# Strassen's form for the second products of the second MLP of a fused attention and MLP kernel

## The chip, the cores and the metric

The kernel runs on one core of one Trainium2 chip. The metric is the device time of one execution in microseconds. All of the work, from the inputs in HBM to the result in HBM, is one launch.

## The reference, cut to what matters

The change is in the last step of the reference. x comes from an attention step and a first MLP and has 4 batches of 576 tokens with 512 features each. The weights of the second MLP are w_ch1 (512 x 1536) and w_ch2 (1536 x 512); w_tok1 and w_tok2 mix the tokens ahead of it.

```python
def _moe2_ref(x, w_tok1, w_tok2, w_ch1, w_ch2):
    xt = x.transpose(0, 2, 1)
    h = np.maximum(xt @ w_tok1, 0.0) @ w_tok2
    u = x + h.transpose(0, 2, 1)
    h2 = np.maximum(u @ w_ch1, 0.0) @ w_ch2
    return (u + h2).astype(np.float32)
```

## The kernel before, in words

**Tiling.** The 2304 tokens are 18 tiles of 128 and 9 chunks of two tiles (CT = 2, CN = 256 tokens). The chunks are numbered 0 to 8 in the first MLP and 9 to 17 in the second (NCH = 9), so chunk 9 is the first one of the second MLP. The hidden features are cut into units of 128: 16 units per chunk in the first MLP (UA), 12 in the second (UB). `seq` lists all units in order as pairs (chunk, unit).

**Precision.** An operand of a product is held as two fp32r numbers, a high part and the low part that is left, and a product is three matmuls: high by high, high by low, low by high (PASSES). In the tiles the index of the part is 0 for high and 1 for low.

**One unit.** `g1(i)` (L875) makes the unit's 128 hidden features for 256 tokens: 4 blocks of input features by 3 passes, 12 matmuls of 256 columns into a bank of PSUM ("h", two banks). `relu(i)` (L884, ScalarE) writes the high part, `low(i)` (L888, VectorE) the low part into the tile "ht". `g2(i)` (L901) multiplies them by the unit's 128 rows of w_ch2: 2 tiles of tokens by 3 passes, 6 matmuls of 512 columns, which add to two banks `acc[c, 0]` and `acc[c, 1]` over the 12 units of the chunk. `chunk_end` adds the banks to u (`evac`, L914, VectorE) and stores the two tiles.

**Order.** Up to unit 111 the order of all instructions is written out by hand. Behind it, from the later part of the first MLP on, the loop at the end of `block_kernel` emits for each unit i: `g1`, `relu`, `low` of unit i+1, then what was `put` at unit i, then `g2(i)`. A planner with a simulated timeline then sets the order of each engine's instructions from that; each engine and the DMA queue of SP run them in that order.

**Work around the units.** `w_load` and `w_split` bring the second MLP's weights (double precision in HBM, "st", L298) and convert them (L257 to L275) one unit ahead of chunk 9's use; `put_tok` places a batch's token products: `xs_load` (L970, a DMA of a tile of x into the tile xr), `xs_split` (L976 ScalarE, L977 GpSimd, into the tile xs), `tok1` (L992), `tok_relu` (L1001, L1002). `put_prep2` places `u_load`, `tok2` (L1023, added to u in L1028) and the turning of u into the operand of `g1` (L810, L818, L830, L835). `close_att` gives the attention's memory to the pools of this part.

Of the kernel before, what the change touches and what calls it, by code (L numbers as in the profile page):

```python
# [197 lines left out]
def block_kernel(ctx: ExitStack, tc: tile.TileContext, qk, vw, vh, vg, g_ln, wa, t1, t2, wb, band, near, lv, edge, out):  # L198
# [24 lines left out]
    ident = const.tile([128, 128], F32, name="ident")  # L223
    identr = const.tile([128, 128], F32R, name="identr")
    maskr = [const.tile([128, NTL, k], F32R, name=f"maskr{k}") for k in (KW, KB)]
    grow = const.tile([128, DM], F32, name="grow")
# [706 lines left out]
    PW = 512 + 3 * 64

    def load_tok(i):
        if i == 0:
            tokw["t1"] = tok["pool"].tile([128, 2, NTL, DT], F32R, tag="t1w", name="t1w")
            tokw["t2"] = tok["pool"].tile([128, 2, 2, PW], F32R, tag="t2w", name="t2w")
            for a in range(2):
                nc.vector.memset(f32(tokw["t2"][:, a, :, 512:576]), 0.0)  # L940
# [56 lines left out]
    def tok_relu(b):  # L997
        r = wp.tile([128, DT // 128, 2, DM], F32R, tag="w", name="r")
# [13 lines left out]
    def tok2(c, j):  # L1012
# [323 lines left out]
```

## Time and profile before

| | |
|---|---|
| time, three runs | 885.16, 886.54, 889.37 us (median 886.54) |
| time of the profiled execution | 886.56 us |
| its span, first to last instruction | 884.8 us |
| TensorE busy | 863.8 us (98%), 6418 matmuls |
| VectorE busy | 518.4 us (59%) |
| ScalarE busy | 251.4 us (28%) |
| GpSimd busy | 193.6 us (22%) |
| mean granted clock of TensorE | 0.998 |

Busy time is the union of an engine's instructions. PE is TensorE's matmuls, PEld its weight loads, DVE is VectorE, ACT ScalarE, POOL GpSimd, SP the engine that issues the DMAs. A name with q is the engine's sequencer, which waits or issues. L875 is line 875 of the kernel. In an instruction, out<-in are the names of the tiles. Matmuls overlap, so that the time from start to start is less than the duration of one.

### The profile page before, as it was taken

The page shows a single profiled execution, that of the slowest core. Times are in us where ns is not written, and L with a number is a line of the kernel's source. Part 1 is how long each engine was busy: PE and PEld are TensorE (multiplying, and loading weights), DVE is VectorE, ACT ScalarE, POOL GpSimd, SP SyncE. Part 2 cuts the span into 40 slices and gives each one's busy share as a digit, 9 for nine tenths or more (in the row PEclk, how much of TensorE's full clock was granted, in tenths as well). Part 3 has the DMA queues.
Part 4 walks back from the last instruction along what each step waited for, and adds up shares of the span by engine and source line. Part 5 has one row for each costly group of instructions (what it writes and reads, how often), then busy time and mean ns, then how long its engine had stood idle before and what let it go on. Part 6 is the DMA issues. An engine that isn't in the chain of part 4 may idle for free.

```text
span 884.8 us, 16767 instructions
## 1 busy us (share of the span) xinstructions
PE 863.8 (98%) x6418; PEld 766.3 (87%) x6418; DVE 518.4 (59%) x1114; ACT 251.4 (28%) x713; POOL 193.6 (22%) x197
## 2 busy tenths in 40 slices
PE   7999999999999999999999999989999999999998
PEld 6888899887989999989999887879898898999997
DVE  5999999999998776832222779863213232222221
ACT  5665535354322111322111233222121111111111
POOL 7731323566873510111000000110010000000000
PEclk9999999999999999999999999999999999999999
DMA  9747776578662522532111356632222121121100
GB/s 280 193 151 225 225 237 199 148 199 224 168 150 72 139 49 60 175 92 89 36 37 48 107 155 178 193 115 53 52 56 46 29 67 35 17 45 23 31 24 24
DMA packets 126752, 98.39 MB, mean 111 GB/s; under 512 B 78744, under 2 KB 104376, under 8 KB 126672
## 3 DMA queue, kind: packets, MB, share of 16 engines
q1 hardware_dynamic: 126672, 97.31, 39.4%
q8 instruction: 51, 0.84, 0.4%
q14 instruction: 29, 0.24, 0.1%
HBM read 72.87 MB, written 16.53 MB: 101 GB/s over the span
## 4 chain that ended last, share of the span: by engine, by line
PE 66%; DVE 19%; DMA 8%; SPq 3%; issue 2%; POOL 1%; ACT 1%; DVEq 0%; ACTq 0%; POOLq 0%
PE h L875 30%; PE acc L901 27%; DMA xr<-x_scr 3%; DMA st<-in_wb_dram 3%; SPq L818 3%; PE k L901 2%; DVE cv L267 2%; PE g L1023 2%; DVE ht L888 1%; DVE cv L262 1%; DVE lp L718 1%; DVE la L726 1%; DVE cv L257 1%; PE k L992 1%; DMA up_scr<-od 1%
## 5 line engine op out<-in xcount | busy, mean ns | idle before, releaser
L875 PEld LDWEIGHTS h<-xt,w 128*128 128x128 f32 x3024 | 394.2, 191 | 22.9 <-DVE ht L888 2.1
L875 PE MATMUL h<-xt,w 128*128 128x256 f32 x3024 | 404.8, 284 | 1.4 <-DVE ht L888 1.3
L901 PE MATMUL acc<-w,ht 128*128 128x512 f32 x1416 | 367.7, 395 | 3.0 <-DVE ht L888 2.4
L901 PEld LDWEIGHTS acc<-w,ht 128*128 128x128 f32 x1416 | 253.5, 189 | 52.3 <-DVE ht L888 4.6
L888 DVE SCALAR_TENSOR_TENSOR ht<-h,ht 128x256 fp32r<-128x256 f32 x252 | 105.6, 419 | 273.4 <-ACT ht L884 273.0
L884 ACT ACTIVATE ht<-h 128x256 fp32r<-128x256 f32 x252 | 96.7, 384 | 439.0 <-PE h L875 355.8
L977 POOL TENSOR_TENSOR xs<-xr,xs 128x512 fp32r<-128x512 f32 x20 | 26.5, 1323 | 293.3 <-ACT xs L976 293.3
L272 ACT ACTIVATE w<-cv 128x512 fp32r<-128x512 f32 x56 | 35.5, 635 | 66.6 <-DVE cv L267 66.5
L684 POOL TENSOR_TENSOR lp<-lqk 128x576 f32<-128x576 f32 x28 | 40.4, 1444 | 43.2 <-DVE ls L690 31.5
L275 DVE TENSOR_TENSOR w<-cv,w 128x512 fp32r<-128x512 f32 x56 | 42.8, 767 | 4.3 <-ACT w L272 4.1
L267 DVE SCALAR_TENSOR_TENSOR cv<-st,cv 128x512 int32<-128x512 int32 (+4 forms) x63 | 44.2, 703 | 0.4
L655 POOL TENSOR_TENSOR x<-x,et 128x256 f32<-128x256 f32 (+2 forms) x40 | 32.0, 820 | 50.6 <-DMA et<-loc_scr 40.0
L262 DVE SCALAR_TENSOR_TENSOR cv<-st,cv 128x512 int32<-128x512 int32 (+4 forms) x63 | 41.5, 659 | 0.4
L257 DVE TENSOR_SCALAR cv<-st 128x512 int32<-128x512 int32 (+4 forms) x63 | 27.3, 433 | 15.2 <-DMA st<-in_wb_dram 10.5
L455 POOL TENSOR_TENSOR vg<-vg 72x256 f32<-72x256 f32 x39 | 31.4, 806 | 18.3 <-DMA vg<-in_vg_dram 15.3
L992 PE MATMUL k<-xs,t1w 128*128 128x512 f32 (+1 forms) x120 | 32.1, 406 | 2.6 <-ACT xs L976 1.9
L1023 PE MATMUL g<-r,t2w 128*128 128x512 f32 x120 | 34.0, 394 | 0.0
L830 ACT ACTIVATE xt<-xt 128x512 fp32r<-128x512 f32 x30 | 18.9, 631 | 34.6 <-DMA xt<-xc 31.2
L835 DVE TENSOR_TENSOR xt<-xt 128x512 fp32r<-128x512 f32 x30 | 24.1, 803 | 7.3 <-ACT xt L830 7.0
L901 PE MATMUL k<-w,ht 128*128 128x512 f32 x96 | 26.0, 403 | 0.1
L992 PEld LDWEIGHTS k<-xs,t1w 128*128 128x128 f32 (+1 forms) x120 | 19.2, 188 | 7.9 <-ACT xs L976 2.8
L1023 PEld LDWEIGHTS g<-r,t2w 128*128 128x128 f32 x120 | 20.9, 189 | 3.0
(189 smaller groups left out, 656.4 us busy)
## 6 DMA issues: line engine op xcount, KB each, us to landing
st<-in_wa_dram SPq DMA_DIRECT2D x28, 512.0 KB
st<-in_wb_dram SPq DMA_DIRECT2D x24, 512.0 KB
xt<-xc SPq DMA_DIRECT2D x480, 16.0 KB
qk<-in_qk_dram SPq DMA_DIRECT2D x13, 581.0 KB
x_scr<-x SPq DMA_DIRECT2D x18, 256.0 KB
x<-x_scr SPq DMA_DIRECT2D x9, 512.0 KB
out_dram<-x SPq DMA_DIRECT2D x18, 256.0 KB
xr<-x_scr SPq DMA_DIRECT2D x16, 256.0 KB
```

The lines of the kernel that those rows point to most:

```text
L257: return nc.vector.tensor_scalar(out=f, in0=h, scalar1=3, scalar2=0x3FFFFFFF, op0=ALU.logical_shift_left, op1=ALU.bitwise_and)
L262: nc.vector.scalar_tensor_tensor(out=f, in0=h, scalar=-0x40000000, in1=f, op0=ALU.bitwise_and, op1=ALU.bitwise_or)
L267: nc.vector.scalar_tensor_tensor(out=f, in0=l, scalar=29, in1=f, op0=ALU.logical_shift_right, op1=ALU.bitwise_or)
L272: nc.scalar.activation(out=hi, in_=f.bitcast(F32), func=ACTF.Copy)
L275: nc.vector.tensor_tensor(out=lo, in0=f.bitcast(F32), in1=f32(hi), op=ALU.subtract)
L684: nc.gpsimd.tensor_tensor(out=t["pr"], in0=t["qk"][:, :VQ], in1=t["qk"][:, VQ + D * o:VQ + D * o + VQ], op=ALU.mult)
L875: nc.tensor.matmul(out=hp[:, :CN], lhsT=w[:, 0, a, kk * 128:(kk + 1) * 128], rhs=xT[c][:, kk, e, :], start=(n == 0), stop=(n == 3 * KD - 1),)
L884: nc.scalar.activation(out=t[:, 0], in_=hps[i][:, :CN], func=ACTF.Relu)
L888: nc.vector.scalar_tensor_tensor(out=t[:, 1], in0=hp[:, :CN], scalar=0.0, in1=f32(t[:, 0]), op0=ALU.max, op1=ALU.subtract)
L901: nc.tensor.matmul(out=acc[c, j], lhsT=t[:, a, j * 128:(j + 1) * 128], rhs=w[:, 1, e, :], start=(m == 0 and n == 0), stop=(last and n == 2),)
L992: nc.tensor.matmul(out=rps[b, m], lhsT=tokw["t1"][rows, a, n, m * 128:(m + 1) * 128], rhs=t[rows, e, :], start=(n == 0 and i == 0), stop=( ...
L1023: nc.tensor.matmul(out=ps, lhsT=tokw["t2"][:, a, m, o:o + 128], rhs=r_t[b][:, m, e, :], start=(i == 0), stop=(i == len(ops) - 1),)
```

## The change

In the second MLP, from chunk 10 on, units 1 to 10 are taken as five pairs. With A the four blocks of relu(u w_ch1) (two tiles of tokens by two units) and B the four blocks of w_ch2 (two units by two halves of 256 output features), the eight block products of a pair become the seven of Strassen's form (as Winograd wrote it): four of A's operands and four of B's are sums of blocks. Units 0 and 11 of a chunk, and all of chunk 9, stay as they are.

`tq_sums` makes the sums of B once for each pair, beside chunks 9 and 10; `pair_sums` makes those of A for each pair of each chunk and splits all seven operands into high and low; `g1_pair` makes both units' first products in one bank; `g2_pair` makes the seven products, which add to the two banks acc and, for the four that belong to more than one output block, to two banks of "g"; `mix` adds these two banks to u at the end of the chunk. To make room, constants of the attention move into its pool, xr is dropped (a load goes into the second half of the tile xs and is split in place), the buffers of x and u are shared out anew, `tok_relu` reuses two tiles, the zero columns of the token weights get narrower, `tok2` uses the banks "k", and batches 2 and 3 of the token products are placed three units later.

The diff, cut to its core:

```diff
+FAST = 11
+QF = DM // 2
...
     def relu(i):
-        hT[i] = t = ht_p.tile([128, 2, CN], F32R, tag="ht", name="ht")
+        if i < base[NCH + 1]:
+            t = ht_p.tile([128, 2, CN], F32R, tag="ht", name="ht")
+        else:
+            t = tok["h2"].tile([128, 2, 7, 128], F32R, tag="h7", name="h7", bufs=2)
+            t = t[:, :, :2].rearrange("p e j n -> p e (j n)")
+        hT[i] = t
...
+    def fast(i):
+        c, m = seq[i]
+        return c > NCH and 0 < m < FAST
+
+    def tq_open():
+        for k in range(2):
+            t = wp.tile([128, 4, 2, QF], F32R, tag="w", name="tw")
+            free.extend(t[:, q] for q in range(3 + k))
+            if k == 0:
+                nc.vector.memset(f32(t[:, 3, 1]), 0.0)
+                z = t.rearrange("p q e n -> p (q e) n")
+                tq["z"] = [z[:, 0::7], z[:, 2::5]]
...
+    def tq_sums(m):
+        b = []
+        s = tok["pool"].tile([128, 2, DM], F32, tag="xs", name="ts", bufs=2)
+        for k in (m, m + 1):
+            w = wt[UA + k]
+            t = s[:, k - m]
+            nc.vector.tensor_copy(t[:, 0:1], gate[0])
+            nc.gpsimd.tensor_tensor(out=t, in0=f32(w[:, 1, 0]), in1=f32(w[:, 1, 1]), op=ALU.add)
+            b.append(t)
+        (b11, b12), (b21, b22) = ((t[:, :QF], t[:, QF:]) for t in b)
+        for o, x, y in ((b11, b12, b11), (b12, b22, b12), (b22, b22, b11), (b21, b21, b22)):
+            nc.vector.tensor_tensor(out=o, in0=x, in1=y, op=ALU.subtract)
...
+        tq[m] = [wt[UA + m][:, 1, :, QF:]] + [free.pop(0) for _ in range(3)]
+        for t, v in zip(tq[m], (b11, b22, b12, b21)):
+            nc.scalar.activation(out=t[:, 0], in_=v, func=ACTF.Copy)
+            nc.vector.tensor_tensor(out=t[:, 1], in0=v, in1=f32(t[:, 0]), op=ALU.subtract)
+
+    def g1_pair(i):
+        hp = ps_h.tile([128, 2, CN], F32, tag="h", name="h")
+        for k in range(2):
+            c, m = seq[i + k]
+            w = wunit(c, m)
+            for n, (kk, a, e) in enumerate([(kk, a, e) for kk in range(KD) for a, e in PASSES]):
+                nc.tensor.matmul(
+                    out=hp[:, k], lhsT=w[:, 0, a, kk * 128:(kk + 1) * 128], rhs=xT[c][:, kk, e, :],
+                    start=(n == 0), stop=(n == 3 * KD - 1),
+                )
+        hps[i] = hp
+
+    def pair_sums(i):
+        hp = hps.pop(i)
+        t = hT[i] = tok["h2"].tile([128, 2, 7, 128], F32R, tag="h7", name="h7", bufs=2)
+        f = tok["h2"].tile([128, 7, 128], F32, tag="hf", name="hf")
+        for k in range(2):
+            nc.scalar.activation(
+                out=f[:, 2 + 2 * k:4 + 2 * k].rearrange("p j n -> p (j n)"), in_=hp[:, k], func=ACTF.Relu
+            )
+        for o, x, y, op in (
+            (0, 3, 5, ALU.add), (1, 0, 2, ALU.subtract), (3, 2, 3, ALU.subtract), (6, 4, 1, ALU.subtract),
+        ):
+            nc.vector.tensor_tensor(out=f[:, o], in0=f[:, x], in1=f[:, y], op=op)
+        for o in (slice(0, 4), slice(4, 7)):
+            hi, lo, v = (x[:, o].rearrange("p j n -> p (j n)") for x in (t[:, 0], t[:, 1], f))
+            nc.scalar.activation(out=hi, in_=v, func=ACTF.Copy)
+            nc.vector.tensor_tensor(out=lo, in0=v, in1=f32(hi), op=ALU.subtract)
+        gate[0] = f32(t[:, 1, 4, 0:1])
+
+    def g2_pair(i):
...
+        if m == 1:
+            for k in (2, 3):
+                acc[c, k] = psg("g")
+        for a_, w, k, o in (
+            (1, t2, 2, lo), (2, wx[:, :, lo], 2, hi), (3, t3, 3, lo), (0, t1, 3, hi),
+            (4, wy[:, :, lo], 0, lo), (6, wy[:, :, hi], 0, hi), (5, t4, 1, lo),
+        ):
+            for n, (a, e) in enumerate(PASSES):
+                first = m == 1 and n == 0 and k > 1 and o == lo
+                nc.tensor.matmul(
+                    out=acc[c, k] if first else acc[c, k][:, o], lhsT=t[:, a, a_],
+                    rhs=tq["z"][k - 2] if first else w[:, e],
+                    start=first, stop=(m == FAST - 2 and n == 2 and k > 1 and o == hi),
+                )
+
+    def mix(i):
+        c, m = seq[i]
+        u = uch[c]
+        ga, gb = acc.pop((c, 2)), acc.pop((c, 3))
+        p, z = (x_p.tile([128, DM], F32, tag="xc", name="xc", bufs=2) for _ in range(2))
+        nc.scalar.activation(out=p[:, :QF], in_=ga[:, QF:], func=ACTF.Copy)
+        nc.scalar.activation(out=p[:, QF:], in_=gb[:, QF:], func=ACTF.Copy)
+        nc.vector.tensor_tensor(out=z[:, :QF], in0=ga[:, :QF], in1=p[:, :QF], op=ALU.add)
+        nc.vector.tensor_tensor(out=z[:, QF:], in0=gb[:, :QF], in1=z[:, :QF], op=ALU.add)
+        nc.gpsimd.tensor_tensor(out=u[:, 0], in0=u[:, 0], in1=p, op=ALU.add)
+        h = u[:, 1].rearrange("p (k n) -> p k n", k=2)
+        nc.vector.tensor_tensor(
+            out=h, in0=h, in1=z[:, QF:].unsqueeze(1).to_broadcast([128, 2, QF]), op=ALU.add
+        )
+        nc.gpsimd.tensor_tensor(out=u[:, 1, QF:], in0=u[:, 1, QF:], in1=p[:, QF:], op=ALU.add)
+        nc.vector.tensor_tensor(out=u[:, 0, QF:], in0=u[:, 0, QF:], in1=z[:, :QF], op=ALU.add)
...
     def xs_load(b, n):
-        t = tok["pool"].tile([128, DM], F32, tag="xr", name="xr", bufs=1)
+        t = xs[b, n] = tok["pool"].tile([128, 2, DM], F32R, tag="xs", name="xs", bufs=2)
+        d = f32(t[:, 1])
...
-            nc.sync.dma_start(out=t, in_=x2_scr[k // CT][:, k % CT])
-        xs[b, n] = t
+            nc.sync.dma_start(out=d, in_=x2_scr[k // CT][:, k % CT])
 
     def xs_split(b, n):
-        r = xs[b, n]
-        t = tok["pool"].tile([128, 2, DM], F32R, tag="xs", name="xs", bufs=2)
-        nc.scalar.activation(out=t[:, 0], in_=r, func=ACTF.Copy)
-        nc.gpsimd.tensor_tensor(out=t[:, 1], in0=r, in1=f32(t[:, 0]), op=ALU.subtract)
-        xs[b, n] = t
+        t = xs[b, n]
+        nc.scalar.activation(out=t[:, 0], in_=f32(t[:, 1]), func=ACTF.Copy)
+        nc.gpsimd.tensor_tensor(out=t[:, 1], in0=f32(t[:, 1]), in1=f32(t[:, 0]), op=ALU.subtract)
...
-        t = x_p.tile([128, CT, DM], F32, tag="x", name="x")
+        t = x_p.tile([128, CT, DM], F32, tag="x", name="x", bufs=3)
         nc.sync.dma_start(out=t, in_=x2_scr[c - NCH])
         uch[c] = t
...
-    put_tok(2, base[NCH + 2])
-    put_tok(3, base[NCH + 4])
...
+    put_tok(2, base[NCH + 2] + 3)
+    put_tok(3, base[NCH + 4] + 3)
+    bf = base[NCH]
+    put(bf + 2, tq_open)
+    put(bf + 2, rota.__setitem__, slice(None), ["k"])
+    for m in range(1, FAST, 2):
+        put(bf + m + 8, tq_sums, m)
+    put(bf + 10, h2_open)
+
+    items, i = [], UNITS
+    while i < NSEQ:
+        items.append((i, 2 if fast(i) else 1))
+        i += items[-1][1]
+    for (i, n), (k, q) in zip(items, items[1:] + [(0, 0)]):
+        for f in ((), (g1, relu, low), (g1_pair, pair_sums))[q]:
+            f(k)
+        for j in range(i, i + n):
+            for f in mid[j]:
+                f()
+        if n == 2:
+            g2_pair(i)
+            if not fast(i + n):
+                with tc.high_priority(offset=HP2):
+                    mix(i)
+        else:
+            g2(i)
+            chunk_end(i)
+        for j in range(i, i + n):
+            for f in bg[j]:
+                f()
```

## Rows read from the trace of the kernel before

**Rows 1.** The page, and windows: busy us (instructions) by engine, granted clock, DMA.
```profile
PE 863.8 (98%) x6418; PEld 766.3 (87%) x6418; DVE 518.4 (59%) x1114; ACT 251.4 (28%) x713; POOL 193.6 (22%) x197
...
core 0: us, PE busy (x) PEld busy (x) DVE busy (x) ACT busy (x) POOL busy (x), PEclk, DMA share, GB/s
...
560.00:600.00 40.00, 36.77 (x206) 30.07 (x206) 27.56 (x46) 10.94 (x23) 7.11 (x5) 1.00 0.47 143
600.00:640.00 40.00, 40.00 (x245) 35.83 (x244) 11.53 (x23) 7.81 (x18) 2.58 (x2) 1.00 0.23 56
...
840.00:885.00 45.00, 40.61 (x257) 36.46 (x255) 8.52 (x18) 5.38 (x14) 0.00 (x0) 1.00 0.07 24
```

**Rows 2.** The chain of waits near its end: start us, us, what.
```profile
851.13 2.75 PE acc L901 x12
...
877.87 2.54 PE acc L901 x11
```

**Rows 3.** Timeline of PE, 742 to 764: start us, us, instructions in one block.
```profile
746.63 3.04 PE L875 MATMUL h<-xt,w 128*128 128x256 f32 x24
749.50 2.91 PE L901 MATMUL acc<-w,ht 128*128 128x512 f32 x12
752.25 1.59 PE L875 MATMUL h<-xt,w 128*128 128x256 f32 x12
...
760.71 1.59 PE L875 MATMUL h<-xt,w 128*128 128x256 f32 x12
762.14 1.55 PE L901 MATMUL acc<-w,ht 128*128 128x512 f32 x6
763.53 1.59 PE L875 MATMUL h<-xt,w 128*128 128x256 f32 x12
```

**Rows 4.** Groups of weight loads, 560 to 885: busy us, mean ns.
```profile
L875 PEld LDWEIGHTS h<-xt,w 128*128 128x128 f32 x1211 | 158.9, 191 | 9.9 <-ACT w L272 0.9 <-DVE ht L888 0.4 <-issue 0.4
```

**Rows 5.** Groups by line and shape: busy us, mean ns of one.
```profile
L884 ACT ACTIVATE ht<-h 128x256 fp32r<-128x256 f32 x101 | 38.6, 382 | 208.3 <-PE h L875 194.1 <-PE acc L901 14.2
L976 ACT ACTIVATE xs<-xr 128x512 fp32r<-128x512 f32 x9 | 5.7, 630 | 16.3 <-DMA xr<-x_scr 15.9 <-PE k L992 0.4
L551 DVE TENSOR_TENSOR x<-acc,pt 64x128 f32<-64x128 f32 x2 | 0.5, 274 | 0.0
...
L551 DVE TENSOR_TENSOR x<-acc,pt 128x256 f32<-128x256 f32 x4 | 1.6, 412 | 0.0
...
L888 DVE SCALAR_TENSOR_TENSOR ht<-h,ht 128x256 fp32r<-128x256 f32 x102 | 43.1, 423 | 181.7 <-ACT ht L884 181.7
...
L835 DVE TENSOR_TENSOR xt<-xt 128x512 fp32r<-128x512 f32 x15 | 10.2, 680 | 5.9 <-ACT xt L830 5.7
L977 POOL TENSOR_TENSOR xs<-xr,xs 128x512 fp32r<-128x512 f32 x9 | 12.3, 1364 | 110.0 <-ACT xs L976 110.0
```

**Rows 6.** Timeline near 587: an instruction of DVE beside one of POOL.
```profile
586.58 1.30 POOL L977 TENSOR_TENSOR xs<-xr,xs 128x512 fp32r<-128x512 f32 x1 [4.41 <-ACT xs L976]
587.06 1.37 DVE L275 TENSOR_TENSOR w<-cv,w 128x512 fp32r<-128x512 f32 x1 [0.96 <-ACT w L272]
```

**Rows 7.** Timeline of PE, 572 to 584: in brackets idle us before, and its releaser.
```profile
573.28 0.72 PE L992 MATMUL k<-xs,t1w 128*128 128x512 f32 x2 [0.33 <-ACT xs L976]
...
580.79 0.73 PE L992 MATMUL k<-xs,t1w 128*128 128x512 f32 x2 [1.61 <-ACT xs L976]
...
582.22 1.19 PE L992 MATMUL k<-xs,t1w 128*128 128x512 f32 x4 [0.69 <-POOL xs L977]
```

**Rows 8.** Timeline, 876 to 886: the end.
```profile
877.70 2.91 PE L901 MATMUL acc<-w,ht 128*128 128x512 f32 x12
...
880.42 1.29 DVE L914 TENSOR_TENSOR x<-acc,x 128x512 f32<-128x512 f32 x2 [1.68 <-PE acc L901]
```

**Rows 9.** Waits of SP's queue, 490 to 620: us in total, times, longest.
```profile
SPq L970 <- POOL xs L977: 8.7, 4, 2.5
```

More of the change, by code (lines that the diff above doesn't have):

```diff
@@ L221, in block_kernel @@
     x2_scr = [dram.tile([128, CT, DM], F32, name=f"x2_scr{c}") for c in range(NCH)]
[L223 to L226, printed above, removed]
+    ident = at.tile([128, 128], F32, name="ident")
+    identr = at.tile([128, 128], F32R, name="identr")
+    maskr = [at.tile([128, NTL, k], F32R, name=f"maskr{k}") for k in (KW, KB)]
+    grow = const.tile([128, DM], F32, tag="grow", name="grow")
     POOLS = {"acc": ps_acc, "h": ps_h, "g": ps_g, "k": ps_k}
@@ L860, in block_kernel @@
     seq += [(c, m) for c in range(2, 2 * NCH) for m in range(nunits(c))]
+    NSEQ = len(seq)
+    base = [0]
+    for c in range(2 * NCH):
+        base.append(base[-1] + nunits(c))
     hT = {}
@@ L890, in low @@
         )
+        if i > UNITS:
+            gate[0] = f32(t[:, 1, 0:1])
     def g2(i):
@@ L927, in chunk_end @@
                     store(i, j)
+    tq = {}
+    free = []
+    gate = [None]
+    def fast(i):
[10 more added lines that the diff above has]
+        for k in range(2):
+            t = x_p.tile([128, 2, 2, QF], F32R, tag="x2", name="tx", bufs=2)
+            free.extend(t[:, q] for q in range(2))
+        free.append(tok["pool"].tile([128, 2, QF], F32R, tag="tq", name="tq"))
+        free.append(const.tile([128, 2, QF], F32R, tag="grow", name="tg"))
@@ new lines, in g1_pair @@
+    def g1_pair(i):
+        hp = ps_h.tile([128, 2, CN], F32, tag="h", name="h")
+        for k in range(2):
+            c, m = seq[i + k]
[6 more added lines that the diff above has]
+        hps[i] = hp
@@ new lines, in pair_sums @@
+    def pair_sums(i):
+        hp = hps.pop(i)
+        t = hT[i] = tok["h2"].tile([128, 2, 7, 128], F32R, tag="h7", name="h7", bufs=2)
+        f = tok["h2"].tile([128, 7, 128], F32, tag="hf", name="hf")
+        for k in range(2):
+            nc.scalar.activation(
[10 more added lines that the diff above has]
+        gate[0] = f32(t[:, 1, 4, 0:1])
@@ new lines, in g2_pair @@
+    def g2_pair(i):
+        c, m = seq[i]
+        t = hT.pop(i)
+        wx, wy = (wunit(c, m + k)[:, 1] for k in range(2))
+        t1, t2, t3, t4 = tq[m]
+        lo, hi = slice(0, QF), slice(QF, DM)
+        if m == 1:
[12 more added lines that the diff above has]
+                )
@@ L997, in tok_relu @@
     def tok_relu(b):
[L998 removed]
+        if b < 2:
+            r_t[b] = r_t[b + 2] = wp.tile([128, DT // 128, 2, DM], F32R, tag="w", name="r")
+        r = r_t[b]
         for m in range(DT // 128):
@@ L1016, in tok2 @@
         elif n == 4:
-            parts = [(2 * g, 576), (2 * g + 1, 512)]
+            parts = [(2 * g + 1, 512), (2 * g, 576)]
         else:
@@ L1028, in tok2 @@
         nc.vector.tensor_tensor(out=u, in0=ps, in1=u, op=ALU.add)
-    NSEQ = len(seq)
     bg = {i: [] for i in range(NSEQ)}
     mid = {i: [] for i in range(NSEQ)}
-    base = [0]
-    for c in range(2 * NCH):
-        base.append(base[-1] + nunits(c))
     def put(pos, f, *args):
@@ L1201, in block_kernel @@
         put_prep2(c, base[c] - 1)
-    put_tok(2, base[NCH + 2])
-    put_tok(3, base[NCH + 4])
-    for i in range(UNITS, NSEQ):
-        if i + 1 < NSEQ:
-            for f in (g1, relu, low):
-                f(i + 1)
-        for f in mid[i]:
-            f()
-        g2(i)
-        chunk_end(i)
-        for f in bg[i]:
-            f()
+    put_tok(2, base[NCH + 2] + 3)
[27 more added lines that the diff above has]
+                f()
 def _bands():
```

22 lines of the change are left out of this document (15 added, 7 removed).

## The prediction

> **What bounds the kernel now.** I read four views in this order. First the page and its windows [rows 1]: TensorE is busy 98% of the span at a granted clock of 1.00, the level of 2.4 GHz, and from 600 us to the last products it is never idle (40.00 us of work in 40 us). VectorE has 8.5 us (in the last 45) to 11.5 us (in the first 40) of work there, ScalarE 5.4 to 7.8, GpSimd at most 2.6. All eight chunks that the change touches (10 to 17) run in that stretch. Second, the end of the chain of waits [rows 2]: one block of matmuls follows the other, with no transfer and no other engine between them. A nanosecond taken off a matmul there is a nanosecond off the span, so long as no other engine comes in between. Third, TensorE's timeline, for the price of the two kinds of block. Fourth, the stretch 560 to 600, chunk 9, which is different: VectorE is busy 27.6 of 40 us, TensorE 36.8.
>
> **The products.** A pair of units now makes 24 first products of 256 columns and 12 second products of 512. In [rows 3] 24 first products take 749.50 − 746.63 = 2.87 us from start to start, 119.6 ns each; 12 second products take 752.25 − 749.50 = 2.75 us, 229.2 ns each. After the change a pair makes 21 second products of 256 columns (seven block products, three precision passes), each with a 128-column weight load, the same form as a first product. At 119.6 ns they take 2.51 us, 0.24 us less. With 8 chunks of 5 pairs: 40 × 0.238 = 9.5 us saved. In each chunk two of these products are widened to 512 columns to open a whole bank: 16 × (229.2 − 119.6) = 1.75 us given back. Net **−7.8 us**. Bounds: by the steady unit in [rows 3], 763.53 − 760.71 = 2.82 us, a pair is 5.64 and becomes 45 × 0.1196 = 5.38, which gives 0.26 × 40 − 1.75 = −8.6. If a second product carries more fixed time than a first one (six take 1.39 us, 231.7 ns; less the 219.2 ns that two lots of 109.6 ns for 256 columns make, 12.5 ns stay, so 122.1 ns for 256 columns), it is 40 × (2.75 − 2.56) − 1.75 = −5.7. I take −7.8, as the blocks of the form itself show it.
>
> What speaks against this is the number of weight loads: 21 in the place of 12, and a single load is recorded with 191 ns [rows 4], longer than a narrow matmul's 119.6 ns step. But first products have one load each too and step at 119.6, so loads overlap each other and the matmuls. The Trainium skill, "TensorE: Matmul & The Clock Gate", section "Back-to-back issue gap", says that load and matmul set the spacing together and states about 81 ns per matmul at 128 columns and 131 at 512. Interpolated, an estimate from that page, 256 columns would cost 98 ns: 21 × 98 − 12 × 131 = +0.49 us a pair, a change that loses some 19 us. The trace disagrees with both figures (119.6 and 229.2 ns for 256 and 512 columns).
>
> **The sums of h (pair_sums).** They replace two pairs of relu and low. Prices [rows 5]: relu of 256 columns 0.38 us, a copy of 512 0.63 us; a VectorE sum of two blocks of 128 columns about 0.27 (the 128-column row, on 64 partitions) and at most 0.41 (the 256-column row); the low parts 0.68 us for 512 columns and about 0.55 for 384. After the last first product the chain is 0.38 + 3 × 0.27 + 0.63 + 0.68 = 2.5 us to the first four low parts (2.9 at 0.41). Its cover is the pair before's second products (2.51 us) and the next first products: 2.87 us, or 1.43 before unit 11. So 3.9 us of cover at the least, and I cost it at nothing. VectorE's load rises by 4 × 0.27 + 0.68 + 0.55 − 2 × 0.42 = 1.5 us a pair, from about 10 to 18 us of 40. If the cover were gone, each 0.1 us of it would cost 4 us in 40 pairs.
>
> **The sums of the weights (tq_sums).** Five times, from nine units into chunk 9 on: two GpSimd sums of 512 columns (1.36 us each [rows 5]), four VectorE sums and four low parts of 256 columns (0.41 and 0.42), four copies (0.38). That is 3.3 us of VectorE each, with a latency near 2.7 + 1.6 + 2.0 = 6.3 us, against four units, some 11 us, until TensorE needs them. But chunk 9's VectorE is nearly full until 588, and a two-input VectorE instruction that falls beside a GpSimd one takes twice its time: L275 took 1.37 us at 587.06 against 0.68, with GpSimd busy 586.58 to 587.88 [rows 6]. In chunk 10 a pair has 2.3 us of pair_sums, 3.3 us of weight sums and other work in 5.4 us of TensorE. What queues behind a weight sum on VectorE are low parts, and TensorE waits for those. Lower bound nothing; upper bound half a sum's 3.3 us at each of two places, 3 us. I take **+0.7 us**.
>
> **The token loads (xs_load).** The buffer xr, of which there was one, is gone: a load goes straight into the split pair's second half, of which there are two. Before, load n+1 waits for GpSimd's split of n; the three TensorE stalls of chunk 9 that come from it are 0.33 + 1.61 + 0.69 = 2.6 us [rows 7]. After, load n+2 waits for TensorE's product of n, so a load can run one ahead. The wait now stands in SP's queue before the loads of weights (L298), which chunk 9 needs just in time: those wait with it, and after them the conversion that w_split emits. So the bounds are −2.6 us (the stalls go) and, by the same rows, +2.6 (as much comes back behind late weights). I take **−0.7**.
>
> **The last recombination (mix).** In chunks 10 to 16 it hides under unit 11 and the next chunk's first products; the next chunk takes the two banks of acc only 1.43 + 1.39 + 2.87 = 5.7 us later. In chunk 17 it stands before the last two evac: before, these end at 881.71, 1.1 us after the last matmul [rows 8]. The banks of mix are complete 9 matmuls (1.1 us) before the last pair ends, and the last six second products take 1.39 us more. From that completion: two copies 0.76, GpSimd's sum of 512 columns 1.36, a VectorE sum 0.42, evac 0.68 twice, with 0.2 of delivery, 4.1 us, against 1.08 + 1.39 + 1.1 = 3.6 us before. That is +0.5; with VectorE held by GpSimd for the 0.68 us above, +1.2; if mix can only start when the pair is done, +1.6. I take **+0.8**.
>
> **At nothing:** tok2 on the other two banks (TensorE is full there in any case), one narrower zero strip, token products moved three units later, two r tiles reused, three buffers in the place of five for u (a buffer's store is 10 units old when it is loaded again). If one were uncovered, it would be one transfer, 2 to 4 us. No DMA is added.
>
> **Sum** against the profiled execution's own 886.56 us (span 884.8; the median of the runs shown, 886.54, is the same): 886.56 − 7.8 + 0.7 − 0.7 + 0.8 = **879.6 us**.
>
> **Rivals.** *The opening gains*: in chunk 9 loads run ahead and the weight sums hide. −8.6 − 2.6 + 0.8 gives 876.2 at best, 877 in the middle. For it: the loads' waits in [rows 7]; against it: VectorE's load there. *The opening loses*: SP's queue stands behind a token load, the weights are late, weight sums crowd the low parts: −7.8 + 2.6 + 3 + 0.8 gives 885.2 at worst, 883.5 in the middle. For it: weights just in time; against it: the same queue is held by GpSimd's splits for 8.7 us now [rows 9]. *Low parts set the pace* (other side): TensorE waits at each pair for pair_sums. From 7.0 / 40 = 0.18 us a pair on nothing is gained; at 0.4 us the time is 895.6. Against it: 3.9 us of cover for 2.5. *Loads set the pace* (other side): a narrow matmul with its own load costs more than half of a wide one. The point of decision is (2.75 − 0.04 − 0.02) / 21 = 128 ns (0.04 and 0.02 are a pair's share of the widened products and of the end); if the recorded 191 ns were the step, 40 × (21 × 0.191 − 2.75) = +50 us, some 937; at 140 ns 40 × 0.19 + 16 × 0.09 + 0.8 = +9.8, 896. Only at 119.6 does the trace show this form. The page of the Trainium skill named above is a rule of this kind.
>
> **Chances.** Forecast 0.62 (876.5 to 882.5), opening gains 0.12, opening loses 0.15, low parts 0.07, loads 0.04. A measurement of this kernel can tell about 0.5%, 4.4 us, so faster means under 882.1: 0.60 + 0.12 + 0.04 = 0.76. The same: most of "opening loses" and the weak forms of the last two, 0.16. Slower, over 891: 0.08. The range takes both openings in: 875.5 to 885.5.
>
> **What would show it.** Second products of chunk 11 on at 120 ns a step and a chunk 1.0 us shorter, without idle time between blocks; idle before them released by VectorE's low parts would be the third rival. Two widened products per chunk at 229 ns. In chunk 9, TensorE's idle time before L992, and what SP's queue waits for, decide between the openings. At the end, the last evac some 2 us after the last matmul. Wrong would be a step over 125 ns, or stalls at chunk ends.

## The result, and the profile after

The changed kernel took 895.34 us (median of 5 runs, 894.14 to 899.04), the kernel before 885.18 on the same chip: ratio 1.0112, 95% interval 1.0081 to 1.0143. It is about 10 us slower, where 7 us faster was forecast. The profiled execution took 894.14 us (span 892.43).

Stretches of the changed kernel's trace, in the columns of [rows 1] (busy us of PE, PEld, DVE, ACT, POOL, then granted clock and DMA):

```profile
560.00:600.00 40.00, 31.70 (x186) 26.85 (x185) 34.52 (x71) 13.36 (x29) 5.80 (x4) 0.96 0.39 118
600.00:640.00 40.00, 36.74 (x268) 34.78 (x267) 32.10 (x72) 16.37 (x41) 14.83 (x11) 0.96 0.18 48
640.00:680.00 40.00, 40.00 (x294) 37.30 (x293) 23.09 (x50) 14.74 (x34) 7.71 (x6) 1.00 0.31 86
...
800.00:840.00 40.00, 40.00 (x315) 38.82 (x314) 21.83 (x51) 13.36 (x31) 2.04 (x2) 1.00 0.19 42
```

Against [rows 1], TensorE has lost 5.1 us of work in the first stretch and 3.3 in the second, and its granted clock fell in both. VectorE is busy 34.5 and 32.1 of 40 us, for 27.6 and 11.5. From 640 on TensorE has no idle time to speak of.

There the products do what was forecast. Timeline of PE in chunk 16, one pair:

```profile
803.01 3.04 PE L991 MATMUL h<-xt,w 128*128 128x256 f32 x24
805.89 0.40 PE L1030 MATMUL g<-tw,h 128*128 128x256 f32 x2
...
808.35 3.03 PE L991 MATMUL h<-xt,w 128*128 128x256 f32 x24
```

The 21 second products run from 805.89 to 808.35, 117 ns each, and follow the 24 first ones without a gap. The pair takes 5.34 us; in [rows 3] two units take 5.64.

Other work was pushed back, though. Matmuls of the token products (tok1 and tok2, 512 columns, about 0.23 us each) from the first product of chunk 10 on, counted by the view of groups, in the kernel before (from 586.4 us):

```profile
L1023 PE MATMUL g<-r,t2w 128*128 128x512 f32 x60 | 17.0, 394 | 0.0
L992 PE MATMUL k<-xs,t1w 128*128 128x512 f32 (+1 forms) x36 | 9.6, 408 | 0.0
```

and in the changed kernel (from 586.8 us):

```profile
L1147 PE MATMUL k<-r,t2w 128*128 128x512 f32 (+1 forms) x66 | 17.6, 395 | 0.0
L1112 PE MATMUL k<-xs,t1w 128*128 128x512 f32 (+1 forms) x60 | 15.4, 416 | 0.0
```

Of 96 it has become 126: 24 more first token products and six more second ones, 30 × 0.23 = 6.9 us. Batch 2's 30 first products ran at 567 to 588 us, 24 of them in chunk 9, and now run at 626 to 671. Chunk 10 starts at 586.8 us as it did at 586.4, with less done.

The second loss is idle time and a lower clock. Windows from chunk 10's first product to the last matmul of the changed kernel:

```profile
586.80:592.00 5.20, 3.47 (x26) 3.18 (x25) 5.05 (x15) 2.43 (x6) 0.00 (x0) 0.97 0.09 14
592.00:600.00 8.00, 8.00 (x50) 7.64 (x49) 6.13 (x16) 3.35 (x8) 2.52 (x2) 0.81 0.32 87
600.00:620.00 20.00, 19.68 (x159) 19.05 (x158) 17.03 (x43) 9.21 (x23) 6.02 (x4) 1.00 0.19 43
620.00:640.00 20.00, 17.06 (x110) 15.73 (x110) 15.06 (x31) 7.17 (x19) 8.81 (x7) 0.91 0.17 53
640.00:887.00 247.00, 246.94 (x1883) 235.62 (x1881) 131.03 (x298) 81.15 (x188) 23.42 (x20) 1.00 0.19 46
```

Up to 640 TensorE is idle for 1.73 + 0.32 + 2.94 = 5.0 us; the clock takes (1 − 0.81) × 8 + (1 − 0.91) × 20 + 0.03 × 5.2 = 3.5 us more, as stretches at the 1.2 GHz level. The same stretch of the kernel before has 0.2 us of idle time and a granted clock of 1.00 throughout.

The budget of the two profiled executions from chunk 10 to the last matmul is 300.1 us against 294.2. Of the difference, 5.9 us, 6.9 are token products and 8.3 idle time and clock, so the pairs took 9.3 us off. By their own steps it should be some 10: 40 × 0.30 − 1.75.

Where the idle time comes from, two stretches show. Timeline, 582 to 591 us (in brackets the idle time before and its releaser):

```profile
582.36 3.28 POOL L972 TENSOR_TENSOR ts<-w 128x512 f32<-128x512 f32 x2 [47.34 <-DVE ts L971]
582.80 1.72 DVE L269 SCALAR_TENSOR_TENSOR cv<-st,cv 128x512 int32<-128x512 int32 x1
...
585.23 3.17 PE L881 MATMUL h<-xt,w 128*128 128x256 f32 x24 [1.16 <-ACT w L274]
...
590.13 0.73 PE L914 MATMUL acc<-w,ht 128*128 128x512 f32 x2 [1.73 <-ACT w L274]
```

The first weight sums stand among the last weight conversions. L269 takes 1.72 us beside GpSimd, 0.69 alone, and TensorE waits for converted weights. Over the whole of chunk 9, though, TensorE is idle for 6.9 us here (4.1 in the kernel before) and also for 6.9 us in the run without weight sums below: in chunk 9 the sums add none. Then, 621 to 626 us, a pair of chunk 10 beside the last of the weight sums:

```profile
621.65 3.08 DVE L1008 TENSOR_TENSOR hf<-hf 128x128 f32<-128x128 f32 x4
621.83 2.54 POOL L972 TENSOR_TENSOR ts<-w 128x512 f32<-128x512 f32 x2 [6.88 <-DVE ts L971]
...
624.62 1.04 ACT L1011 ACTIVATE h<-hf 128x512 fp32r<-128x512 f32 x2 [4.14 <-DVE hf L1008]
...
625.72 0.77 PE L1030 MATMUL acc<-w,h 128*128 128x256 f32 x2 [2.94 <-ACT h L1011]
```

Four VectorE sums of h with 128 columns take 3.08 us beside GpSimd's sums of weights; two of the four are stretched, to 1.30 and 1.35 us. Everything behind them waits: ScalarE's copies, the low parts, and TensorE for 2.94 us. All 160 of them, by source (least, median, longest ns):

```profile
L1008 DVE TENSOR_TENSOR hf<-hf x160: 274/285/1434, 597.4 to 880.7; 128x128 f32<-128x128 f32 x160
```

The median, 285 ns, is about the 0.27 us that was forecast; the longest is five times as much. Six of the 160 take over 0.3 us, each beside a GpSimd instruction; three of these stand beside weight sums, from 607 to 624 us.

At the end (timeline, 885 to 889 us):

```profile
885.38 1.56 PE L914 MATMUL acc<-w,h 128*128 128x512 f32 x6
885.51 1.29 POOL L1045 TENSOR_TENSOR x<-x,xc 128x512 f32<-128x512 f32 x1 [29.72 <-ACT xc L1042]
885.99 1.36 DVE L1047 TENSOR_TENSOR x<-x,xc 128x512 f32<-128x512 f32 x1
...
887.79 1.29 DVE L927 TENSOR_TENSOR x<-acc,x 128x512 f32<-128x512 f32 x2
```

The last recombination goes on after the last matmul (886.94). The last evac ends 2.14 us behind it, 1.1 us in the kernel before [rows 8]; with the stores the tail is 1.25 us longer, for the 0.8 of the forecast.

### The profile page after: what moved, and what is told of

Same layout as the page of the kernel before. It is cut to its first block, busy times and chain, and to the rows that moved or that the text cites. A ratio compares the mean times of both kernels' runs of the same rounds, so it can differ in the third digit from the quotient of the medians.

```text
span 892.4 us, 18008 instructions
## 1 busy us (share of the span) xinstructions
PE 861.4 (97%) x6778; PEld 778.0 (87%) x6778; DVE 613.8 (69%) x1355; ACT 301.8 (34%) x829; POOL 222.5 (25%) x223
## 4 chain that ended last, share of the span: by engine, by line
PE 66%; DVE 20%; DMA 7%; SPq 3%; issue 2%; ACT 1%; POOL 0%; DVEq 0%; ACTq 0%
PE h L881 18%; PE acc L914 16%; PE h L991 12%; PE g L1030 6%; PE acc L1030 4%; DMA st<-in_wb_dram 3%; SPq L820 2%; DVE cv L269 2%; DVE cv L264 2%; PE k L914 2%; PE k L1112 2%; PE k L1147 2%; DVE cv L259 2%; DVE ht L899 1%; DVE w L277 1%
## 5 line engine op out<-in xcount | busy, mean ns | idle before, releaser
L914 PE MATMUL acc<-w,ht 128*128 128x512 f32 x840 | 221.1, 397 | 9.0 <-ACT w L274 2.8
L914 PEld LDWEIGHTS acc<-w,ht 128*128 128x128 f32 x840 | 149.4, 189 | 41.2 <-DVE ht L899 3.7
L895 ACT ACTIVATE ht<-h 128x256 fp32r<-128x256 f32 x156 | 60.0, 385 | 224.5 <-PE h L881 164.6
L899 DVE SCALAR_TENSOR_TENSOR ht<-h,ht 128x256 fp32r<-128x256 f32 x156 | 65.0, 417 | 92.4 <-ACT ht L895 91.9
L1098 POOL TENSOR_TENSOR xs<-xs 128x512 fp32r<-128x512 f32 x20 | 26.2, 1315 | 255.2 <-ACT xs L1097 255.2
L1008 DVE TENSOR_TENSOR hf<-hf 128x128 f32<-128x128 f32 x160 | 45.6, 323 | 57.0 <-ACT hf L1002 55.7
L1012 DVE TENSOR_TENSOR h<-hf,h 128x512 fp32r<-128x512 f32 x80 | 47.2, 628 | 18.5 <-ACT h L1011 18.5
L1011 ACT ACTIVATE h<-hf 128x512 fp32r<-128x512 f32 x80 | 42.1, 570 | 43.2 <-DVE hf L1008 43.2
L1002 ACT ACTIVATE hf<-h 128x256 f32<-128x256 f32 x80 | 26.2, 380 | 75.8 <-PE h L991 70.6
L657 POOL TENSOR_TENSOR x<-x,et 128x256 f32<-128x256 f32 (+2 forms) x40 | 32.1, 824 | 47.9 <-DMA et<-loc_scr 38.1
L269 DVE SCALAR_TENSOR_TENSOR cv<-st,cv 128x512 int32<-128x512 int32 (+4 forms) x63 | 43.3, 689 | 0.5
L1030 PE MATMUL acc<-w,h 128*128 128x256 f32 x240 | 37.9, 284 | 3.0 <-ACT h L1011 2.9
```

Source lines behind the costliest of these rows:

```text
L269: nc.vector.scalar_tensor_tensor(out=f, in0=l, scalar=29, in1=f, op0=ALU.logical_shift_right, op1=ALU.bitwise_or)
L899: nc.vector.scalar_tensor_tensor(out=t[:, 1], in0=hp[:, :CN], scalar=0.0, in1=f32(t[:, 0]), op0=ALU.max, op1=ALU.subtract)
L914: nc.tensor.matmul(out=acc[c, j], lhsT=t[:, a, j * 128:(j + 1) * 128], rhs=w[:, 1, e, :], start=(m == 0 and n == 0), stop=(last and n == 2),)
L1008: nc.vector.tensor_tensor(out=f[:, o], in0=f[:, x], in1=f[:, y], op=op)
L1011: nc.scalar.activation(out=hi, in_=v, func=ACTF.Copy)
L1012: nc.vector.tensor_tensor(out=lo, in0=v, in1=f32(hi), op=ALU.subtract)
```

## The experiments

Theory 1: the pairs save what was forecast, and the token products and idle time that the rearrangement brings (buffers, banks, order) cost more than that. Theory 2: the weight sums and the sums of h, crowded on VectorE, cost it, and the rearrangement nothing. Theory 3: the pairs themselves save nothing, because of their weight loads or sums of h. Ratios are to the kernel before on the same chip, with the 95% interval; 0.1% is 0.9 us. A difference of two ratios carries an error of some 3 us. In the diffs "after" and "before" mean the kernel that is edited.

**The rearrangement alone** (after; all units ordinary):

```
-        return c > NCH and 0 < m < FAST
+        return False
...
-    for m in range(1, FAST, 2):
-        put(bf + m + 8, tq_sums, m)
```

> All of the change's rearrangement, but no pair and no weight sum: every unit of the second MLP is an ordinary one. Theory 1 (displaced work): in the kernel before, batch 2's token products (30 matmuls, 6.9 us) ran inside chunk 9, where TensorE waits for VectorE's weight conversion anyway; the new sharing of buffers and banks pushes them behind it. Then this kernel, which saves nothing, takes 885.2 + 6.9 = 892 us. Theory 2 (crowding alone: weight sums and pair sums on VectorE cost everything): it takes what the kernel before takes, 885 to 886.

Measured: 896.93 us, 1.0112 [1.0082, 1.0143]. With no pair and no weight sum the kernel loses as much as the change does, some 9.9 us. Its chunk 10 starts at 589.2 us, 2.8 later than before, with these token products behind it:

```profile
L1147 PE MATMUL k<-r,t2w 128*128 128x512 f32 (+1 forms) x66 | 17.9, 394 | 0.0
L1112 PE MATMUL k<-xs,t1w 128*128 128x512 f32 (+1 forms) x60 | 15.6, 403 | 0.0
```

126 as in the changed kernel: 2.8 + 6.9 = 9.7 us. Theory 2 falls as the only cause: the rearrangement is not free. That the whole change takes just as long (1.0112) does not mean that the pairs do nothing: the next run shows that what they save is spent on the weight sums.

**The change without its weight sums** (after; tq holds copies of weight blocks in the place of the sums, so the second MLP's result is another):

```
-            nc.gpsimd.tensor_tensor(out=t, in0=f32(w[:, 1, 0]), in1=f32(w[:, 1, 1]), op=ALU.add)
...
-            nc.vector.tensor_tensor(out=o, in0=x, in1=y, op=ALU.subtract)
...
+        for t in tq[m][1:]:
+            nc.scalar.activation(out=t, in_=f32(wt[UA + m][:, 1, :, :QF]), func=ACTF.Copy)
```

> The changed kernel with its pairs, but the sums of weight blocks are left out: the operands are filled by three ScalarE copies of a weight block per pair, so the output is not the reference's. VectorE and GpSimd lose all of tq_sums. Theory 2 (crowding at 580 to 630 by the weight sums, with the half clock that follows the idle time): about 6 us under the changed kernel's 895, so 889. Theory 1 alone: nothing changes, 894 to 895, since batch 2's token products stay behind chunk 9 as before.

Measured: 891.28 us, 1.0043 [1.0023, 1.0064]. Against the changed kernel, 0.69% less: the weight sums, with the buffers that they take in the ring of xs, cost 6.1 us. Against the rearrangement alone the same 0.69%: 6.1 us is what pairs without weight sums bring, the longer end included. Its windows:

```profile
560.00:600.00 40.00, 33.88 (x192) 27.82 (x191) 29.59 (x57) 17.70 (x36) 1.77 (x1) 0.96 0.42 131
600.00:640.00 40.00, 40.00 (x325) 39.30 (x324) 22.50 (x54) 13.51 (x32) 2.03 (x2) 1.00 0.19 42
```

From 600 on TensorE is full at 1.00: the idle time there was the sums'. The first stretch still shows 33.9 of 40 and 0.96: that part is the rearrangement's. By theory 1 alone this run would have taken as long as the change, so both theories hold a part. Theory 3 falls.

**Batch 2's products moved alone** (before; one VectorE copy makes the batch's first load wait until chunk 10's result is there):

```
+        if (b, n) == (2, 0):
+            nc.vector.tensor_copy(t[:, 0:1], uch[NCH + 1][:, 0, 0:1])
```

> The kernel before with one small VectorE copy that makes the first load of batch 2's tokens wait for chunk 10's result; nothing else differs and no work is left out. Theory 1: its 30 token matmuls move from chunk 9, where they filled time that TensorE waits anyway, to behind it: 885.2 + 6.9 = 892. If TensorE's time in chunk 9 were not spare, moving work changes nothing: 885 to 886.

Measured: 891.16 us, 1.0039 [1.0016, 1.0063], 3.5 us, half of what was expected. Chunk 9 in the kernel before, then here:

```profile
533.60:586.40 52.80, 48.73 (x272) 40.30 (x271) 45.75 (x80) 16.85 (x35) 5.79 (x4) 1.00 0.60 180
```

```profile
532.80:582.80 50.00, 44.79 (x247) 37.07 (x246) 42.58 (x80) 14.54 (x31) 0.00 (x0) 0.97 0.56 169
```

24 of the batch's first products, 24 × 0.23 = 5.5 us, leave the chunk, and it is only 2.8 us shorter: with 42.6 us of VectorE work in 50, TensorE is idle there for 5.2 us (4.1 before), mostly waiting for converted weights and low parts, and its clock is at 0.97. Products in chunk 9 cost about half their time; behind it they cost all of it.

**The loads in place alone** (before; the edit of `xs_load` and `xs_split` as in the change):

```
-        t = tok["pool"].tile([128, DM], F32, tag="xr", name="xr", bufs=1)
+        t = xs[b, n] = tok["pool"].tile([128, 2, DM], F32R, tag="xs", name="xs", bufs=2)
+        d = f32(t[:, 1])
```

> The kernel before with one piece of the rearrangement: the token loads go straight into the second half of the tile xs and wait for TensorE's product two tokens back. If this step makes SP's queue stand, so that the operands of chunk 6 and the weights come late (seen in the changed kernel's trace at 370 to 396 us), it costs 3 to 5 us: 1.004 to 1.006. If loads running ahead is a gain, as the prediction took it, or if SP's order in the changed kernel comes from other pieces, 0.997 to 1.000.

Measured: 892.92 us, 1.0065 [1.0041, 1.009], 5.8 us, for a forecast of −0.7. In the profiled execution part of the time is lost at chunk 6, where batch 0's tokens are loaded, some 150 us before chunk 9, where the forecast looked. SP's queue there, in the kernel before, then here:

```profile
376.49 0.33 SPq L298 DMA_DIRECT2D st<-in_wb_dram  x1
377.68 1.15 SPq L968 DMA_DIRECT2D xr<-x_scr  x2
378.88 10.32 SPq L818 DMA_DIRECT2D xt<-xc  x16
```

```profile
378.23 5.38 SPq L298 DMA_DIRECT2D st<-in_wb_dram  x2
383.66 10.25 SPq L818 DMA_DIRECT2D xt<-xc  x16
```

Two weight loads, issued over 5.4 us, now stand ahead of 16 transfers that turn a tile of x; these begin 4.8 us later. They carry chunk 7's operand, not chunk 6's as the expectation has it (chunk 6's first products run from 383.8 us, while they are still being issued), but chunk 6 suffers. Timeline, 395 to 398 us:

```profile
395.47 0.75 DVE L770 SCALAR_TENSOR_TENSOR xc<-x,mv,grow 128x512 f32<-128x512 f32 x1 [6.33 <-DMA xt<-xc]
...
396.13 0.42 DVE L888 SCALAR_TENSOR_TENSOR ht<-h,ht 128x256 fp32r<-128x256 f32 x1
...
396.61 1.21 PE L901 MATMUL acc<-w,ht 128*128 128x512 f32 x4 [1.34 <-DVE ht L888]
```

VectorE stands 6.33 us for these transfers, which read the buffer that it is to fill; a low part of chunk 6 is queued behind, and TensorE waits for that. Chunk 6 takes 51.1 us for 47.0, of which 1.7 are idle time and some 0.7 are three more token products. The changed kernel's chunk 6 takes 50.8, and its queue holds the same pair of loads there (377.44 to 382.77).

Chunk 6 is not the only place. Chunk 9, in the columns of [rows 1], to be read against the kernel before just above:

```profile
537.10:594.90 57.80, 52.37 (x283) 43.34 (x281) 48.33 (x83) 17.97 (x36) 8.91 (x7) 0.97 0.58 172
```

It takes 5.0 us longer. Eleven more token products are in it, 2.5 us, which came mostly from chunks 7 and 8; the rest is idle time (5.4 us for 4.1) and the lower clock. What starts these stalls is not shown.

**Those loads on GpSimd's queue** (the kernel above, the same loads issued by GpSimd):

```
-            nc.sync.dma_start(out=d, in_=x2_scr[k // CT][:, k % CT])
+            nc.gpsimd.dma_start(out=d, in_=x2_scr[k // CT][:, k % CT])
```

> The kernel before with in-place token loads, as in the run that took 1.0065, but these loads are issued by GpSimd's queue, so that SP's queue never stands behind one. In the planned order SP still has two weight loads ahead of chunk 6's operand transfers, as there, where the kernel before has one. If the loads' own wait in SP's queue is the cause, the time returns to 1.000; if the planned order (the second weight load ahead of the operands) is, it stays near 1.005.

Measured: 890.98 us, 1.0042 [1.0025, 1.0058]. It lies between, and its interval overlaps the one above. SP's queue still holds the two weight loads (379.31 to 383.57) with no token load in it, but chunk 6 takes 48.3 us. So the wait of the token loads in this queue is not the whole cost, and the two weight loads alone do not make chunk 6's loss. In the profiled execution 2.4 us are lost before chunk 6 begins, and chunk 9 takes 53.8 us for 52.8. How much the planner's other order has in the cost, and how much the loads' own wait, stays open.

**xr back in the changed kernel** (after; batches 0 and 1, in another pool):

```
+        if b > 1:
...
+            d = xr[b, n] = sp["pool"].tile([128, DM], F32, tag="xr", name="xr", bufs=1)
```

> The changed kernel with one part undone: batches 0 and 1 of the token loads use a buffer xr of their own as before (in the pool that is closed later), batches 2 and 3 load in place. If the in-place loads cost there what they cost alone (0.65%), it takes 1.0112 - 0.0065 = 1.005; if that cost is absorbed by chunk 9, whose end VectorE's weight conversion sets, 1.011.

Measured: 892.35 us, 1.0054 [1.003, 1.0078]: 0.58% less than the changed kernel, about what the loads cost alone, and chunk 6 is back to 46.9 us. There are still 126 token products behind chunk 9: the loads of batches 0 and 1 are not what moved them.

**Banks, token places and r tiles alone** (before):

```
+        if b < 2:
+            r_t[b] = r_t[b + 2] = wp.tile([128, DT // 128, 2, DM], F32R, tag="w", name="r")
...
-    put_tok(2, base[NCH + 2])
+    put_tok(2, base[NCH + 2] + 3)
...
+    put(base[NCH] + 2, rota.__setitem__, slice(None), ["k"])
```

> The kernel before with another piece: batches 2 and 3 reuse the r tiles of 0 and 1, their products are placed three units later, and tok2 takes the banks k from chunk 9 on. By the displaced-work theory this alone holds batch 2's token products back, as gating them did (1.0039): 1.004. If that order comes from the weight sums' place in the ring of xs, which is not here, 1.000.

Measured: 890.11 us, 1.0044 [1.0023, 1.0064]. The cost came, but not by the way that was expected: batch 2's products stayed in chunk 9 (561 to 588 us). Six second token products moved behind it, and in chunk 10 TensorE waited 1.8 us, ahead of a second token product, for VectorE's part of `tok_relu`. What in the edit moved them is open.

**Three buffers for u alone** (before):

```
+            xch[c] = x_p.tile([128, CT, DM], F32, tag="x" if c % 5 < 3 else "x2", name="x", bufs=3 if c % 5 < 3 else 2)
...
+        t = x_p.tile([128, CT, DM], F32, tag="x", name="x", bufs=3)
```

> The kernel before with the last large piece: the five buffers of x and u split into three and two, u getting three. If a later load of u holds tok2 back out of chunk 9, some 12 matmuls or 2.8 us move behind it, of which about half counts: 1.0015. If buffers don't matter, 1.000. The three pieces together should give the 1.0112 of all rearrangement if they add up and nothing is missing.

Measured: 891.09 us, 1.0043 [1.0021, 1.0064], more than expected. 106 token products are behind chunk 9, for 96: 2.3 of the 3.8 us. In its profiled execution (895.99 us) 6 us are lost before chunk 2, where the granted clock was 0.91 over the first 50 us, so that chunk starts there can't be compared. The three parts alone make 0.65 + 0.44 + 0.43 = 1.52%, the whole rearrangement 1.12%: the intervals do not tell the two apart, and none can be read as its share of the whole.

**Weight sums without GpSimd** (after; the two 512-column sums on VectorE):

```
-            nc.gpsimd.tensor_tensor(out=t, in0=f32(w[:, 1, 0]), in1=f32(w[:, 1, 1]), op=ALU.add)
+            nc.vector.tensor_tensor(out=t, in0=f32(w[:, 1, 0]), in1=f32(w[:, 1, 1]), op=ALU.add)
```

> The changed kernel with GpSimd's ten sums of tq_sums (1.36 to 1.4 us each) done by VectorE (0.68 us each); no other change. VectorE gets 6.8 us more work, but no two-input instruction of VectorE meets GpSimd there (pair sums of 0.28 us were recorded with up to 1.43 us beside it). If GpSimd's hold on VectorE is most of the 6 us that the weight sums cost, this takes 1.005 to 1.008; if VectorE's own work is, it stays at 1.011 or goes to 1.013.

Measured: 893.46 us, 1.0085 [1.0052, 1.0118]. Inconclusive: the interval holds the changed kernel's 1.0112 too. The window of the second stretch:

```profile
600.00:640.00 40.00, 36.83 (x283) 34.92 (x282) 31.73 (x84) 16.48 (x41) 6.05 (x4) 1.00 0.19 51
```

TensorE still loses 3.2 us there (3.3 in the changed kernel), though no sum of h is stretched before 674 us; the two that are, up to 1384 ns, stand beside GpSimd's token splits. VectorE's load alone, which this edit raises by ten sums, can make such idle time. How much of the 6.1 us is GpSimd's hold and how much VectorE's own load is not told apart.

**Pairs from chunk 11** (after; batch 2's products back in chunk 9, an r tile more, weight sums spread over chunk 10):

```
-        return c > NCH and 0 < m < FAST
+        return c > NCH + 1 and 0 < m < FAST
...
-    put_tok(2, base[NCH + 2] + 3)
+    put_tok(2, base[NCH] - 2)
...
-        put(bf + m + 8, tq_sums, m)
+        put(bf + 12 + 1.5 * m, tq_sums, m)
```

> The changed kernel with pairs from chunk 11 on (7 chunks), weight sums spread over chunk 10 (1.5 units apart per unit), batch 2's token products placed in chunk 9 with a result tile of their own. If both theories hold, what is left is the saving of the products, 7 x 0.97 = 6.8 us, less 1.3 us for the end: 885.2 - 5.5 = 880. If pairs cost something at each chunk beside this, 886 or more.

Measured: 887.67 us, 1.0005 [0.9984, 1.0027], no change. Chunk 10 starts 8 us late at 594.6, about 5 of which come back behind it. The late start was not in the expectation; the loads in place, still part of this kernel, may be the cause.

**The same with xr** (the kernel above with `xr` for batches 0 to 2):

```
+        if b == 3:
...
+            d = xr[b, n] = sp["pool"].tile([128, DM], F32, tag="xr", name="xr", bufs=1)
```

> The version with pairs from chunk 11, weight sums in chunk 10 and batch 2 early, with the separate load buffer xr back for batches 0 to 2. That version reached chunk 10 8 us later than the kernel before and then gained 5. If the in-place loads are what made it late, this one takes 0.994 to 0.996 of the kernel before; if it is the rest of the rearrangement, it stays at 1.000.

Measured: 880.96 us, **0.9931 [0.9909, 0.9953]**: faster than both kernels, by 6 us than the kernel before. Its windows:

```profile
560.00:600.00 40.00, 36.48 (x208) 29.41 (x207) 26.82 (x53) 10.41 (x23) 2.97 (x3) 1.00 0.41 121
600.00:640.00 40.00, 40.00 (x271) 36.93 (x270) 29.37 (x71) 14.67 (x36) 8.48 (x7) 1.00 0.20 43
```

The first stretch is as in [rows 1]; in the second VectorE has 29.4 us of work, weight sums among it, and TensorE loses nothing at 1.00. 108 token products are behind chunk 9, and it has 35 pairs for 40. The kernel above differs from it in the token loads alone and has the same number of token products in chunk 9: with the loads in place chunk 6 takes 50.8 us for 46.9 here (0.7 us of it are three more token products), and chunk 9 56.0 for 53.3.

**That kernel without its pairs and weight sums:**

```
-        return c > NCH + 1 and 0 < m < FAST
+        return False
...
-    for m in range(1, FAST, 2):
-        put(bf + 12 + 1.5 * m, tq_sums, m)
```

> The version that took 0.9931, without its pairs and weight sums: every unit is an ordinary one, the rearrangement stays. It prices what the pairs are worth where nothing crowds them. By the prediction's own term, 7 chunks x 0.97 us less 1.25 us at the end is 5.5 us, so this takes 0.9931 + 0.0062 = 0.999 to 1.000. If the version's gain came from its rearrangement, it takes 0.994.

Measured: 890.01 us, 1.0035 [1.0016, 1.0053]. The pairs and their sums are worth 1.04%, 9.2 us, in this arrangement, more than the 5.5 expected; the 7.7 of the steps (35 × 0.30, less 1.5 for 14 widened products and 1.25 for the end) lie within the error of some 2.5 us. The arrangement itself still costs 3.1 us.

## Why the prediction was wrong

**The products: right.** 7.8 us was forecast; the blocks step at 117 ns, and the pairs took 9.3 us off in the profiled execution. The rivals in which loads or low parts set the pace are out: 117 ns is under the 128 of the point of decision, and from 640 us on TensorE is idle for 0.06 of 247 us. Only among the weight sums, at 625 us, did TensorE wait long for `pair_sums` (2.94 us). The Trainium skill's rule on load and matmul ("TensorE: Matmul & The Clock Gate", "Back-to-back issue gap"), whose figures would have made the pairs a loss, is not borne out: the steps are 117 and 229 ns for 256 and 512 columns, for 98 (the estimate in the prediction) and 131 by the page, and the pairs gain.

**"At nothing": the step that failed.** The prediction put the banks of tok2 at nothing because "TensorE is full there in any case", and the token products placed three units later without a reason; it did not ask what work these parts move, and from where. That is the error. Token work that leaves a stretch where TensorE is not full, and lands where it is, costs its whole time there and gives back only a part. [Rows 1] showed that chunk 9 is not full: in 560 to 600 TensorE had 36.8 us of work and VectorE 27.6. Thirty token products, 6.9 us, ended up behind chunk 9; when 24 of them alone move (5.5 us), 3.5 stay net. The term had been given "one transfer, 2 to 4 us" as its worst; the rearrangement with the loads cost 9.9 (measured without pairs). Which of its parts moves batch 2's products is not shown: neither the loads nor the banks, places and r tiles do it alone, and the u buffers alone move only ten token products behind chunk 9.

**The token loads: the sign was wrong.** −0.7 was forecast with ±2.6 for bounds, both from chunk 9's stalls. Alone they cost 5.8 us, at two places. The forecast left out chunk 6, though batch 0's loads run there: SP's queue is one list in planned order, and with the buffer gone two weight loads stand ahead of an operand's transfers, for which VectorE, and behind it TensorE, waits. Between the two kernels with pairs from chunk 11, which differ in these loads alone, chunk 6 is 3.9 us longer with the loads in place and chunk 9 2.7. "The opening loses" named a shared queue, weights behind token loads, for chunk 9 alone, with 2.6 us at worst; that it is this wait which lengthens chunk 9 is not shown.

**The weight sums: undersized.** +0.7 was taken, 3 was the bound; without them the kernel is 6.1 us faster. The mechanism was named, low parts queued behind weight sums and two-input instructions beside GpSimd at twice their time [rows 6]. The bound, half a sum's VectorE time at each of two places, was too small. In the trace a 128-column sum stretches up to five times (0.28 to 1.43 us), two of four in one pair, and TensorE, once idle, came back at a lower clock, which the bound left out. But with the large sums on VectorE TensorE lost as much time there with no stretched sum of h; so whether the stretch or VectorE's load is what was undersized stays open. The Trainium skill, "GPSIMD Engine Reference", "Specifications", says that GpSimd shares its SBUF interfaces with VectorE and contends with VectorE instructions of two SBUF inputs. The trace agrees, with L1008 at 1434 ns beside GpSimd's sum and 285 in the median.

**The end:** +1.25 us for +0.8; its upper case, VectorE's sum held by GpSimd (L1047, 1.36 us), is what happened.

The sum of the measured terms is +9.9 for the rearrangement and loads, +6.1 for the weight sums, +1.25 for the end, and for the products −9.3 by the profiled executions or −7.4 by the medians (the 6.1 us between the two runs above and the end's 1.25): +8.0 or +9.9 us. The profiled executions differ by 7.6, the medians by 10.2. The second sum closes by itself, since its terms are differences of the same runs. Between the two readings of the products' term the intervals, 0.2 to 0.3% each way, do not decide.

Not settled: what makes the banks and the u buffers cost 0.43 to 0.44% each, and how the loads' cost splits into planned order and own wait. All runs with ordinary units alone, whatever they edit, are 0.35 to 1.12% slower than the kernel before; that any new plan loses some of an order that happened to be good is a rival which no run excludes.

## What to carry to other kernels

Read the limit of each stretch before costing work that moves: filler that moves from a stretch with idle TensorE time into a full one costs its whole time there and frees only a part of it (here about half) where it left, even if no instruction is added. Where one planner orders a shared queue, a dropped buffer changes other work in that queue; measure the rearrangement without the new arithmetic first. Helper sums belong where VectorE has room: the same pairs, begun one chunk later, with the weight sums spread out, batch 2 back in chunk 9 and the old load buffer, turned +1.1% into −0.7%. Of these steps only the buffer was measured by itself (from 1.0005 to 0.9931).

## What the hardware showed beyond that

Beside a GpSimd sum of 512 columns (1.3 us), a VectorE sum of 128 columns took up to 1.43 us instead of 0.28, about as long as GpSimd's whole instruction. After idle stretches of 1.16 and 1.73 us the granted clock was 0.81 over 592 to 600 us; in the kernel before, stalls of 1.61 and 0.69 us [rows 7] left it at 1.00 over 560 to 600. After 2.94 us of idle time the changed kernel shows this over the next four microseconds:

```profile
626.00:630.00 4.00, 4.00 (x15) 3.44 (x15) 3.88 (x8) 2.01 (x6) 1.27 (x1) 0.60 0.00 0
```

0.60 is a mixture of the 1.2 and the 2.4 GHz level: 1.6 of the 4 us lost, on top of the idle time. And 256-column products with a weight load each stepped at 117 ns where 119.6 was read from the blocks before.
